# The tail of a two-branch attention kernel: last numerators in a score tile, normalized by chunk halves, half the output rows added while they are evicted

## The chip, the cores and the metric

The kernel runs on one core of a Trainium2 chip. Its engines work side by side and meet through semaphores: TensorE (PE, matmuls and their weight loads), VectorE (DVE), ScalarE (ACT), GpSimd (POOL) and SyncE (SP, which here only issues transfers). Matmul results land in PSUM, eight banks of 2 KB in each of 128 partitions; everything else lives in SBUF. The metric is the device time of one execution in microseconds, a median over several. Times inside an execution are counted from the span's start.

## The reference

One input x of 2048 tokens and 640 columns goes through two attention branches with 32 heads of 20 columns, and a gate per token mixes them:

```python
g = sigmoid((x * gate_w).sum(-1, keepdims=True))
a = A_ref(x, ...)   # linear attention, softmax feature maps, then @ A_wo
b = B_ref(x, ...)   # below, then @ B_wo
return g * a + (1 - g) * b

# B_ref: 4 segments of 512 tokens, in order, for each head
p = softmax(q @ k.T * scale + causal_mask); a_dot = p @ v
a_mem = (phi(q) @ M) / (phi(q) @ z + 1e-6)
o = sig(beta) * a_mem + (1 - sig(beta)) * a_dot
M += phi(k).T @ v; z += phi(k).sum()
```

Both outputs are of the same shape, so the sum of the two last products is formed for each block of 128 tokens (a chunk) and written out in bf16.

## The kernel before

Branch A and the projections of branch B run first. Then a loop goes over 32 steps of branch B, two at a time: segment s = 0 to 3 and group g = 0 to 7 of four heads. The order of the work on every engine is written out by hand: what is emitted first runs first on its engine (`manual_schedule`), and a plan of letters mixes projections and output rows into the steps. Waits come from the tiles: an instruction waits for what it reads, and a new tile from a pool waits until every reader of the tile that had the place is done.

PSUM is split into three pools: `bst`, two score tiles of two banks each (`st_ps`); `bnd`, one tile of two banks (`nda`); `bps`, two tiles of one bank (projections, output halves, transposes).

One step works like this. The scores of four heads go to score tiles (L666), ScalarE takes the exponential into PT tiles (L670), GpSimd clears the triangles above the diagonal (L677). `pv_items` multiplies PT with the values, which carry a column of ones, so numerators and denominators of four query chunks j and four heads i come out side by side in bank 0 of `nda` (L722, 40 matmuls, chunk j has j + 1 parts); `mem_items` puts the memory term for the same chunks into bank 1 (L730, four matmuls). `emit_epi` then works on VectorE: reciprocal of the denominators (L747), times the gates (L749), times the numerators into `td` (L759), and an add of both banks' parts into 80 columns of `oB` (L762), by GpSimd, except in the very last step, where VectorE does it.

The tail starts when the loop is over; the numerators of the last step (number 31, s = 3, g = 7) are still to be done. It makes the outputs of the last segment, chunks n = 0 to 3, each in two halves of 320 columns, written here (n, half). Each half is a sum in one PSUM bank: an identity matmul that puts in the row of branch A, which was formed earlier and lies in SBUF as bf16 (`row_mm`, L936), and five matmuls with `WoB`, one for each block of 128 columns of oB turned around (`turned_mm`, L941). Blocks 0 to 2 of oB were turned by transfers (L890) during the last steps. Block 3 (columns 384 to 511, which needs group 6, step 30) and block 4 (columns 512 to 639, which needs group 7, step 31) are turned on TensorE, and ScalarE copies them to SBUF (`block_tr`, L948 and L949). The order on TensorE before is:

- rows and blocks 0 to 2 of chunks 0 and 1 into the two score tiles, 16 matmuls (`fill`)
- numerators and memory terms of step 31 into `nda`, then its epilogue on VectorE
- block 3: four transposes, ScalarE's copy; (2,0) in a `bps` tile beside it; then block 3 of the five halves that are open
- chunk 3 in `nda`, which the epilogue must have read
- block 4: four transposes, ScalarE's copy; then block 4 of the seven halves that are open
- (2,1) in a `bps` tile, six matmuls

ScalarE and VectorE evict the halves in turn (L952, order (0,0) (0,1) (1,0) (1,1) (2,0) (3,0) (3,1) (2,1)), and SyncE's queue issues five output transfers: chunk 0, chunk 1, (2,0), chunk 3, (2,1).

Of the kernel before, what the change touches and what calls it, by code (L numbers as in the profile page):

```python
# [8 lines left out]
ALU = mybir.AluOpType  # L9
BF16 = mybir.dt.bfloat16  # L10
F32 = mybir.dt.float32
# [4 lines left out]
def kernel(  # L16
# [15 lines left out]
    nc = tc.nc  # L32
# [585 lines left out]
    with ExitStack() as bctx:  # L618
# [95 lines left out]
        def pv_items(st, js):  # L714
            vB = vBs[st.s % 2]

            def piece(j, i):
                if j == 0 and i == 0:
                    st.nda = bnd.tile([P, 2, 512], F32, name="nda")
                nd = st.nda[:, 0, 0:4 * GP].rearrange("p (j i e) -> p j i e", j=4, i=4)  # L720
                for c in range(j + 1):
                    nc.tensor.matmul(nd[:, j, i], lhsT=block(st, c)[:, i, (j - c) * P:(j - c + 1) * P],  # L722
                                     rhs=vB[:, c, 4 * st.g + i, :], start=(c == 0), stop=(c == j))
            return [(0.026 * (j + 1), lambda j=j, i=i: piece(j, i)) for j in js for i in range(4)]

        def mem_items(st):
            g = st.g

            def am(j):
                nc.tensor.matmul(st.nda[:, 1, j * GP:(j + 1) * GP], lhsT=phiq_block(st.s, g, j),  # L730
                                 rhs=Mbd[:, g].rearrange("p i e -> p (i e)"), start=True, stop=True)

            def mz(c):
                Mz = st.nda[:, 1, 4 * GP:5 * GP].rearrange("p (i e) -> p i e", i=4)
                nc.tensor.matmul(Mz, lhsT=phiks[st.s % 2][:, c, 4 * g:4 * g + 4, :],  # L735
                                 rhs=vBs[st.s % 2][:, c, 4 * g:4 * g + 4, :],
                                 start=(c == 0), stop=(c == 3))
            return ([(0.037, lambda j=j: am(j)) for j in range(4) if st.s > 0]
                    + [(0.037, lambda c=c: mz(c)) for c in range(4) if st.s < NSEG - 1]
                    + [(0.0, lambda: emit_epi(st))])  # L740

        def emit_epi(st):
            s, g = st.s, st.g
            n = 2 if s > 0 else 1
            ndv = st.nda[:, 0:n, 0:4 * GP].rearrange("p n (ji e) -> p n ji e", e=DH + 1)
            rec = bw.tile([P, 2, 16], F32, name="rec")
            nc.vector.reciprocal(out=rec[:, 0:n], in_=ndv[:, :, :, DH])  # L747
            recv = rec[:, 0:n].rearrange("p n (j i) -> p n j i", j=4)
            nc.vector.tensor_tensor(out=recv, in0=recv,  # L749
                                    in1=ogs[s][:, 0:n, :, 4 * g:4 * g + 4],  # L750
                                    op=ALU.mult)
            rb = rec[:, 0:n, :, None].to_broadcast([P, n, 16, DH])
            oview = oBs[s][:, :, g * 80:(g + 1) * 80].rearrange("p j (i d) -> p j i d", d=DH)
            if n == 1:
                nc.vector.tensor_tensor(out=oview, in0=ndv[:, 0, :, 0:DH].rearrange("p (j i) d -> p j i d", j=4),
                                        in1=rb[:, 0].rearrange("p (j i) d -> p j i d", j=4), op=ALU.mult)
            else:
                td = bw.tile([P, 2, 16, DH], F32, name="td")
                nc.vector.tensor_tensor(out=td, in0=ndv[:, :, :, 0:DH], in1=rb, op=ALU.mult)  # L759
                tdv = td.rearrange("p n (j i) d -> p n j i d", j=4)  # L760
                eng = nc.vector if st.last else nc.gpsimd
                eng.tensor_tensor(out=oview, in0=tdv[:, 0], in1=tdv[:, 1], op=ALU.add)  # L762
            if s < NSEG - 1:
                mtmp = bw.tile([P, 4, DH + 1], F32, name="mtmp")
                nc.vector.tensor_tensor(  # L765
                    out=mtmp, in0=st.nda[:, 1, 4 * GP:5 * GP].rearrange("p (i e) -> p i e", i=4),
                    in1=CM[:, g, :, :], op=ALU.mult)
                nc.gpsimd.tensor_tensor(out=Msb[:, g], in0=Msb[:, g], in1=mtmp, op=ALU.add)
                nc.gpsimd.tensor_copy(out=Mbd[:, g], in_=Msb[:, g])
# [169 lines left out]
        def turned_mm(n, half, k5s):  # L939
            for k5 in k5s:  # L940
                nc.tensor.matmul(banks[n, half], lhsT=oT4[:, n, k5, :],  # L941
                                 rhs=WoB[:, k5, half * 320:(half + 1) * 320],
                                 start=False, stop=(k5 == KC - 1))

        def block_tr(k5, eng):
            tp = bps.tile([P, 4, P], BF16, name="otp", tag="ps1")
            for n in range(4):
                nc.tensor.transpose(out=tp[:, n, :], in_=oB[:, n, k5 * P:(k5 + 1) * P], identity=ident_b)  # L948
            eng(out=oT4[:, :, k5, :], in_=tp)  # L949

        def out_half(n, half, eng):
            eng(out=rows[first + n][:, half * 320:(half + 1) * 320], in_=banks[n, half])  # L952
            lo = {(0, 1): 0, (1, 1): 0, (2, 0): 0, (3, 1): 0, (2, 1): 320}.get((n, half))
            if lo is not None:
                hs = slice(lo, (half + 1) * 320)
                nc.sync.dma_start(out=out2[(first + n) * P:(first + n + 1) * P, hs], in_=rows[first + n][:, hs])

        def fill(n):
            for half in range(2):
                row_mm(n, half)  # L960
                turned_mm(n, half, range(3))

        fill(0)
        fill(1)
        for w, fn in pv_items(prev, range(4)) + mem_items(prev):
            fn()
        block_tr(3, nc.scalar.copy)
        banks[2, 0] = bps.tile([P, 320], F32, name="o_ps", tag="ps1")
        row_mm(2, 0)
        turned_mm(2, 0, range(3))  # L970
        for n in range(2):
            for half in range(2):
                turned_mm(n, half, (3,))
        turned_mm(2, 0, (3,))
        fin = bnd.tile([P, 2, 512], F32, name="nda")
        for half in range(2):
            banks[3, half] = fin[:, half, 0:320]
            row_mm(3, half)
            turned_mm(3, half, range(4))
        block_tr(4, nc.scalar.copy)  # L980
        engs = (nc.scalar.copy, nc.vector.tensor_copy)
        order = [(0, 0), (0, 1), (1, 0), (1, 1), (2, 0), (3, 0), (3, 1)]
        for n, half in order:
            turned_mm(n, half, (4,))
        banks[2, 1] = bps.tile([P, 320], F32, name="o_ps", tag="ps1")
        row_mm(2, 1)
        turned_mm(2, 1, range(KC))
        for k, (n, half) in enumerate(order + [(2, 1)]):
            out_half(n, half, engs[k % 2])


# [28 lines left out]
```

## Time and profile before

| | us |
|---|---|
| median of 3 runs (329.59 to 329.99) | 329.69 |
| the profiled execution, whole | 329.01 |
| its span, first to last instruction | 327.3 |
| TensorE busy | 309.1 |
| ScalarE busy | 252.2 |
| VectorE busy | 222.5 |
| GpSimd busy | 212.3 |
| first row matmul of the tail (L936) starts | 313.70 |
| first numerator matmul of step 31 starts (L722) | 315.88 |
| first cast of an output half starts (L952) | 321.72 |

The granted TensorE clock was 1.00 in each stretch of the tail. In the timeline rows a number before a name is the start, then the length; `x40` says how many instructions of the same kind the row holds, from the first one's start to the last one's end; matmuls overlap, so the start of the next row says more of a group's cost than its length. Brackets name the engine's idle time before the row and what ended it. In the list of waits a row says who waited for whom, for how long in total, how often, and the longest one.

### The profile page before, as it was taken

Reading aid. Unit: us, or ns where it says so; the run is one execution under the profiler, and the core shown is the slowest. Engines: PE = TensorE matmul, PEld = TensorE weight load, DVE = VectorE, ACT = ScalarE, POOL = GpSimd, SP = SyncE. Lnnn points to the kernel's source line nnn. Section 1 sums busy time; section 2 is a strip of 40 time slices with the busy share of each in tenths; the row PEclk is TensorE's granted clock in tenths of the full one; section 3 lists DMA queues with packets and bytes.
Section 4 is the critical chain, followed back from the end, with each engine's and each line's share of the span. In section 5 each row is a group of like instructions: output and inputs, shape, how many; then the busy total and the mean of one; then the engine's idle time right before and its main releaser. Section 6 shows DMA issues by size and latency. Waiting matters only on the chain.

```text
span 327.3 us, 9498 instructions
## 1 busy us (share of the span) xinstructions
PE 309.1 (94%) x3905; PEld 213.3 (65%) x3908; DVE 222.5 (68%) x444; ACT 252.2 (77%) x321; POOL 212.3 (65%) x311
## 2 busy tenths in 40 slices
PE   7999999999999999889999999999799999999994
PEld 7788878864587788455556666655556666565562
DVE  2577988997798897377768576776566666354552
ACT  4677888148845555799999999999789888898842
POOL 8688699203178789646657676777686768665640
PEclk9999999999999999999999999999999999999999
DMA  7947935790017667756321555642555471432212
GB/s 226 211 105 188 221 97 148 215 362 10 0 35 110 129 110 110 149 105 86 59 56 34 98 57 65 123 84 49 86 91 83 87 135 27 94 80 62 49 63 80
DMA packets 91812, 34.19 MB, mean 104 GB/s; under 512 B 79866, under 2 KB 91770, under 8 KB 91770
## 3 DMA queue, kind: packets, MB, share of 16 engines
q1 hardware_dynamic: 91338, 33.11, 49.4%
q8 instruction: 30, 0.49, 0.7%
q10 hardware_dynamic: 432, 0.49, 0.6%
q14 instruction: 12, 0.10, 0.1%
HBM read 6.42 MB, written 2.62 MB: 28 GB/s over the span
## 4 chain that ended last, share of the span: by engine, by line
PE 39%; ACT 21%; DVE 2%; issue 2%; DMA 1%; SPq 0%; ACTq 0%; DVEq 0%
ACT PT L670 19%; PE st_ps L666 9%; PE proj L800 8%; PE proj L854 6%; PE nda L722 6%; PE proj L539 4%; PE num L440 2%; DMA xTf<-Eq 1%; PE nda L730 1%; PE nda L735 1%; PE st_ps L941 1%; ACT ek L826 1%; DVE oTA L952 0%; ACT oTA L949 0%; PE den L450 0%
## 5 line engine op out<-in xcount | busy, mean ns | idle before, releaser
L670 ACT ACTIVATE PT<-st_ps 128x1024 bf16<-128x1024 f32 x160 | 154.0, 1025 | 15.5 <-PE st_ps L666 13.0
L677 POOL TENSOR_SCALAR_AFFINE_SELECT PT<-PT 128x512 bf16<-128x512 bf16 (+1 forms) x130 | 87.0, 687 | 49.1 <-ACT PT L670 48.8
L722 PEld LDWEIGHTS <-PT 128*128 128x128 bf16 x1280 | 40.1, 96 | 11.2 <-issue 6.5
L722 PE MATMUL nda<-vB,PT 128*128 128x21 bf16 x1280 | 42.8, 173 | 1.5 <-DVE mtmp L765 1.3
L244 POOL TENSOR_TENSOR EkSn<-Ek,krec 128x1280 bf16<-128x1280 bf16 x16 | 37.5, 2359 | 8.3 <-DVE krec L243 8.1
L854 PEld LDWEIGHTS <-xTf 128*128 128x128 bf16 x300 | 26.3, 97 | 16.0 <-issue 7.2
L860 DVE CAST Z<-proj 128x320 bf16<-128x320 f32 x44 | 20.8, 486 | 20.1 <-PE proj L854 19.8
L232 PEld LDWEIGHTS <-xTf 128*128 128x128 bf16 x240 | 27.1, 113 | 6.2 <-DVE xTf L197 0.7
L240 DVE TENSOR_REDUCE ksum<-Ek 128x64 f32<-128x1280 bf16 x16 | 23.6, 1474 | 8.1 <-ACT Ek L236 8.1
L236 ACT ACTIVATE Ek<-pk 128x640 bf16<-128x640 f32 x32 | 20.8, 702 | 10.6 <-PE pk L232 9.8
L666 PE MATMUL st_ps<-Z 32*128 32x512 bf16 (+3 forms) x256 | 24.6, 299 | 4.3 <-ACT PT L670 3.1
L486 DVE TENSOR_TENSOR tt<-num,rr 128x640 f32<-128x640 f32 x32 | 24.8, 802 | 4.9 <-POOL rr L479 2.2
L592 POOL TENSOR_TENSOR oA<-tt 128x640 bf16<-128x640 f32 x16 | 24.6, 1546 | 4.6 <-DVE tt L486 3.4
L800 PE MATMUL proj<-WkA,oTA 128*128 128x320 bf16 x160 | 27.1, 299 | 0.0
L666 PE MATMUL st_ps<-Eq 32*128 32x512 bf16 (+3 forms) x256 | 24.5, 299 | 2.2 <-ACT PT L670 1.7
L762 POOL TENSOR_TENSOR oB<-td 128x320 bf16<-128x320 f32 x23 | 19.8, 863 | 6.9 <-DVE td L759 6.9
L398 ACT ACTIVATE Eq<-pq 128x1024 bf16<-128x1024 f32 x20 | 19.4, 1021 | 5.4 <-PE pq L393 5.4
L800 PE MATMUL proj<-WvA,oT 128*128 128x320 bf16 x120 | 22.2, 300 | 0.5 <-DVE oTA L809 0.5
L393 PE MATMUL pq<-xTf,WqA 128*128 128x512 bf16 x97 | 21.9, 379 | 0.2
L759 DVE TENSOR_TENSOR td<-nda,rec 128x640 f32<-128x640 f32 x24 | 19.8, 825 | 2.2
L539 PEld LDWEIGHTS <-xTf 128*128 128x128 bf16 x180 | 16.3, 97 | 4.4
L747 DVE RECIPROCAL rec<-nda 128x32 f32<-128x32 f32 (+1 forms) x32 | 10.6, 330 | 12.4 <-PE nda L730 6.5
(152 smaller groups left out, 558.1 us busy)
## 6 DMA issues: line engine op xcount, KB each, us to landing
Z<-EkSn SPq DMA_DIRECT2D x32, 160.0 KB, 2.7
out_dram<-orow SPq DMA_DIRECT2D x8, 160.0 KB, 2.0
out_dram<-oTA SPq DMA_DIRECT2D x7, 160.0 KB, 1.9
WvA<-in_A_wqkv_dram SPq DMA_DIRECT2D x2, 400.0 KB, 6.6
WkB<-in_B_wk_dram SPq DMA_DIRECT2D x1, 800.0 KB
WqB<-in_B_wq_dram SPq DMA_DIRECT2D x1, 800.0 KB, 6.8
WvB<-in_B_wv_dram SPq DMA_DIRECT2D x1, 800.0 KB, 8.4
WkA<-in_A_wo_dram SPq DMA_DIRECT2D x1, 800.0 KB, 11.1
```

Source lines behind the costliest of these rows:

```text
L232: nc.tensor.matmul(ps[:, bk, 0:n], lhsT=key_tokens(c, sc), rhs=rhs, start=(c == 0), stop=(c == KC - 1))
L240: nc.vector.tensor_reduce(out=ksum, in_=Ek.rearrange("p s (h f) -> p (s h) f", f=DH), axis=AX.X, op=ALU.add)
L244: nc.gpsimd.tensor_tensor(out=EkSn[:, sc].rearrange("p s (h f) -> p (s h) f", f=DH), in0=Ek.rearrange("p s (h f) -> p (s h) f", f=DH), in1 ...
L486: nc.vector.tensor_tensor(out=tt[:, sgn].rearrange("p (b h) d -> p b h d", b=2), in0=ps, in1=csb, op=ALU.mult)
L539: nc.tensor.matmul(ps, lhsT=xq[:, sc // 4, cc, sc % 4 * P:(sc % 4 + 1) * P], rhs=W[:, cc, half * 320:(half + 1) * 320], start=(cc == 0), s ...
L592: nc.gpsimd.tensor_tensor(out=oA.rearrange("p (h d) -> p h d", d=DH), in0=tt[:, 0], in1=tt[:, 1], op=ALU.add)
L666: nc.tensor.matmul(ps[:, i - i0, o:o + L - c * P], lhsT=kT[32 * i:32 * i + 32, c * P:(c + 1) * P], rhs=qT[32 * i:32 * i + 32, c * P:L], st ...
L670: nc.scalar.activation(out=PT[:, i0:i0 + 2], in_=ps, func=ACT.Exp, scale=SCALE_B)
L677: nc.gpsimd.affine_select(out=v, in_=v, pattern=[[0, n_i], [1, P]], compare_op=ALU.is_ge, fill=0.0, base=0, channel_multiplier=-1)
L722: nc.tensor.matmul(nd[:, j, i], lhsT=block(st, c)[:, i, (j - c) * P:(j - c + 1) * P], rhs=vB[:, c, 4 * st.g + i, :], start=(c == 0), stop= ...
L800: nc.tensor.matmul(ps, lhsT=oT[:, k % KC], rhs=W[:, k % KC, hs], start=(k == 0), stop=(k == n - 1))
L854: nc.tensor.matmul(ps, lhsT=xq[:, sc // 4, k, sc % 4 * P:(sc % 4 + 1) * P], rhs=W[:, k, half * 320:(half + 1) * 320], start=(k == 0), stop ...
```

## The change

All of it is in the tail and in the epilogue of step 30.

- The last step's numerators and memory terms go to the second score tile (`prev.nda = pair_ps[1]`) and not to `nda`. They come after chunk 0's seven matmuls and not after the sixteen of chunks 0 and 1. Chunk 0 of the numerators goes first, then chunks 1 to 3 for heads 0 and 1, then for heads 2 and 3.
- Chunk 1's halves go to the `nda` tile that step 30 had, after the memory terms.
- Step 30's add moves from GpSimd to VectorE.
- The last epilogue (`epi_last`) forms `td` and the sum into oB in two parts, query chunks 0 and 1, then 2 and 3.
- The transposes of block 4 come in two pairs with a copy for each. They lie in bank 0 of a score tile that takes the place of the last numerators, and (3,1) in its bank 1. (3,0) takes a `bps` tile.
- (2,1) takes the `nda` tile after chunk 1.
- For (0,1), (1,1), (3,0) and (2,1) there is no identity matmul; VectorE adds the row of branch A while it evicts. The other four halves keep theirs and are copied by ScalarE. The order of the evictions and their engines are as before.
- Chunk 3's output is issued by ScalarE's queue.

```diff
--- before.py
+++ after.py
@@ -715,7 +715,7 @@
             vB = vBs[st.s % 2]
 
             def piece(j, i):
-                if j == 0 and i == 0:
+                if j == 0 and i == 0 and not st.last:
                     st.nda = bnd.tile([P, 2, 512], F32, name="nda")
                 nd = st.nda[:, 0, 0:4 * GP].rearrange("p (j i e) -> p j i e", j=4, i=4)
                 for c in range(j + 1):
@@ -758,7 +758,7 @@
                 td = bw.tile([P, 2, 16, DH], F32, name="td")
                 nc.vector.tensor_tensor(out=td, in0=ndv[:, :, :, 0:DH], in1=rb, op=ALU.mult)
                 tdv = td.rearrange("p n (j i) d -> p n j i d", j=4)
-                eng = nc.vector if st.last else nc.gpsimd
+                eng = nc.vector if s == NSEG - 1 and g == G - 2 else nc.gpsimd
                 eng.tensor_tensor(out=oview, in0=tdv[:, 0], in1=tdv[:, 1], op=ALU.add)
             if s < NSEG - 1:
                 mtmp = bw.tile([P, 4, DH + 1], F32, name="mtmp")
@@ -948,45 +948,92 @@
                 nc.tensor.transpose(out=tp[:, n, :], in_=oB[:, n, k5 * P:(k5 + 1) * P], identity=ident_b)
             eng(out=oT4[:, :, k5, :], in_=tp)
 
-        def out_half(n, half, eng):
-            eng(out=rows[first + n][:, half * 320:(half + 1) * 320], in_=banks[n, half])
-            lo = {(0, 1): 0, (1, 1): 0, (2, 0): 0, (3, 1): 0, (2, 1): 320}.get((n, half))
-            if lo is not None:
-                hs = slice(lo, (half + 1) * 320)
-                nc.sync.dma_start(out=out2[(first + n) * P:(first + n + 1) * P, hs], in_=rows[first + n][:, hs])
-
-        def fill(n):
-            for half in range(2):
+        def epi_last(st):
+
+            s, g = st.s, st.g
+            ndv = st.nda[:, 0:2, 0:4 * GP].rearrange("p n (ji e) -> p n ji e", e=DH + 1)
+            rec = bw.tile([P, 2, 16], F32, name="rec")
+            nc.vector.reciprocal(out=rec, in_=ndv[:, :, :, DH])
+            recv = rec.rearrange("p n (j i) -> p n j i", j=4)
+            nc.vector.tensor_tensor(out=recv, in0=recv, in1=ogs[s][:, :, :, 4 * g:4 * g + 4], op=ALU.mult)
+            td = bw.tile([P, 2, 16, DH], F32, name="td")
+            oview = oBs[s][:, :, g * 80:(g + 1) * 80].rearrange("p j (i d) -> p j i d", d=DH)
+            for j in (0, 2):
+                ji = slice(4 * j, 4 * j + 8)
+                nc.vector.tensor_tensor(out=td[:, :, ji], in0=ndv[:, :, ji, 0:DH],
+                                        in1=rec[:, :, ji, None].to_broadcast([P, 2, 8, DH]), op=ALU.mult)
+                tdv = td[:, :, ji].rearrange("p n (j i) d -> p n j i d", j=2)
+                nc.vector.tensor_tensor(out=oview[:, j:j + 2], in0=tdv[:, 0], in1=tdv[:, 1], op=ALU.add)
+
+        SUMMED = {(0, 1), (1, 1), (3, 0), (2, 1)}
+
+        def fill(n, half, k5s):
+
+            own = (n, half) not in SUMMED
+            if own:
                 row_mm(n, half)
-                turned_mm(n, half, range(3))
-
-        fill(0)
-        fill(1)
-        for w, fn in pv_items(prev, range(4)) + mem_items(prev):
+            for k5 in k5s:
+                nc.tensor.matmul(banks[n, half], lhsT=oT4[:, n, k5, :],
+                                 rhs=WoB[:, k5, half * 320:(half + 1) * 320],
+                                 start=(k5 == 0 and not own), stop=(k5 == KC - 1))
+
+
+        prev.nda = pair_ps[1]
+        for half in range(2):
+            fill(0, half, range(3))
+        for w, fn in pv_items(prev, (0,)):
             fn()
+        later = pv_items(prev, (1, 2, 3))
+        for i0 in (0, 2):
+            for j in range(3):
+                for i in (i0, i0 + 1):
+                    later[4 * j + i][1]()
+        for w, fn in mem_items(prev)[:4]:
+            fn()
+        epi_last(prev)
+        first_nda = bnd.tile([P, 2, 512], F32, name="nda")
+        for half in range(2):
+            banks[1, half] = first_nda[:, half, 0:320]
+            fill(1, half, range(3))
         block_tr(3, nc.scalar.copy)
         banks[2, 0] = bps.tile([P, 320], F32, name="o_ps", tag="ps1")
-        row_mm(2, 0)
-        turned_mm(2, 0, range(3))
-        for n in range(2):
-            for half in range(2):
-                turned_mm(n, half, (3,))
-        turned_mm(2, 0, (3,))
-        fin = bnd.tile([P, 2, 512], F32, name="nda")
-        for half in range(2):
-            banks[3, half] = fin[:, half, 0:320]
-            row_mm(3, half)
-            turned_mm(3, half, range(4))
-        block_tr(4, nc.scalar.copy)
-        engs = (nc.scalar.copy, nc.vector.tensor_copy)
-        order = [(0, 0), (0, 1), (1, 0), (1, 1), (2, 0), (3, 0), (3, 1)]
-        for n, half in order:
+        fill(2, 0, range(3))
+        for n, half in ((0, 0), (0, 1), (1, 0), (1, 1), (2, 0)):
+            turned_mm(n, half, (3,))
+        last_ps = bst.tile([P, 2, L], F32, name="st_ps")
+        tp = last_ps[:, 0].bitcast(BF16)[:, 0:4 * P].rearrange("p (n t) -> p n t", n=4)
+        banks[3, 0] = bps.tile([P, 320], F32, name="o_ps", tag="ps1")
+        banks[3, 1] = last_ps[:, 1, 0:320]
+
+        def last_tr(n):
+            nc.tensor.transpose(out=tp[:, n, :], in_=oB[:, n, 4 * P:KC * P], identity=ident_b)
+
+        last_tr(0)
+        last_tr(1)
+        nc.scalar.copy(out=oT4[:, 0:2, 4, :], in_=tp[:, 0:2])
+        fill(3, 0, range(4))
+        last_tr(2)
+        last_tr(3)
+        nc.scalar.copy(out=oT4[:, 2:4, 4, :], in_=tp[:, 2:4])
+        for n, half in ((0, 0), (0, 1), (1, 0), (1, 1)):
             turned_mm(n, half, (4,))
-        banks[2, 1] = bps.tile([P, 320], F32, name="o_ps", tag="ps1")
-        row_mm(2, 1)
-        turned_mm(2, 1, range(KC))
-        for k, (n, half) in enumerate(order + [(2, 1)]):
-            out_half(n, half, engs[k % 2])
+        fill(3, 1, range(4))
+        for n, half in ((2, 0), (3, 0), (3, 1)):
+            turned_mm(n, half, (4,))
+        banks[2, 1] = bnd.tile([P, 2, 512], F32, name="nda")[:, 0, 0:320]
+        fill(2, 1, range(KC))
+        out_to = {(0, 1): (nc.sync, 0, 0), (1, 1): (nc.sync, 1, 0), (2, 0): (nc.sync, 2, 0),
+                  (3, 1): (nc.scalar, 3, 0), (2, 1): (nc.sync, 2, 320)}
+        for n, half in ((0, 0), (0, 1), (1, 0), (1, 1), (2, 0), (3, 0), (3, 1), (2, 1)):
+            row = rows[first + n][:, half * 320:(half + 1) * 320]
+            if (n, half) in SUMMED:
+                nc.vector.tensor_tensor(out=row, in0=banks[n, half], in1=row, op=ALU.add)
+            else:
+                nc.scalar.copy(out=row, in_=banks[n, half])
+            if (n, half) in out_to:
+                eng, n, lo = out_to[n, half]
+                hs = slice(lo, (half + 1) * 320)
+                eng.dma_start(out=out2[(first + n) * P:(first + n + 1) * P, hs], in_=rows[first + n][:, hs])
 
 
 # ---- launch: one core; inputs and outputs as the reference has them ----
```

## The prediction

> **What bounds the kernel now.** I read the page's head and its chain first, then the timeline from 311 us on, engine by engine, then the waits of that stretch and the transfers.
>
> ```profile
> span 327.3 us, 9498 instructions
> PE 39%; ACT 21%; DVE 2%; issue 2%; DMA 1%; SPq 0%; ACTq 0%; DVEq 0%
> ```
>
> The chain is mostly TensorE (PE) work. The change touches nothing that starts before about 311 us, so only the tail matters. TensorE's rows there (start, length, line, operation, tiles, count):
>
> ```profile
> 313.70 0.30 PE L936 MATMUL st_ps<-oTA,ident_b 128*128 128x320 bf16 x1
> ...
> 315.88 1.16 PE L722 MATMUL nda<-vB,PT 128*128 128x21 bf16 x40
> 316.89 0.31 PE L730 MATMUL nda<-Mbd,xTf 128*128 128x84 bf16 x4
> 317.03 0.39 PE L948 MATMUL otp<-ident_b,oB 128*128 128x128 bf16 x4
> 317.26 0.30 PE L936 MATMUL o_ps<-oTA,ident_b 128*128 128x320 bf16 x1
> ...
> 318.10 0.72 PE L941 MATMUL st_ps<-WvA,oTA 128*128 128x320 bf16 x4
> ...
> 321.24 0.72 PE L941 MATMUL st_ps<-WvA,oTA 128*128 128x320 bf16 x4 [0.68 <-ACT oTA L949]
> ...
> 322.33 0.84 PE L941 MATMUL o_ps<-WvA,oTA 128*128 128x320 bf16 x5
> ```
>
> TensorE is one stream with two holes, each behind a ScalarE copy of transposes (before 318.10 and before 321.24); its last matmul ends at 322.33 + 0.84 = 323.17. Then the other engines:
>
> ```profile
> 312.91 1.68 POOL L677 TENSOR_SCALAR_AFFINE_SELECT PT<-PT 128x256 bf16<-128x256 bf16 x4 [0.26 <-ACT PT L670]
> 314.74 0.82 DVE L759 TENSOR_TENSOR td<-nda,rec 128x640 f32<-128x640 f32 x1
> 315.65 0.86 POOL L762 TENSOR_TENSOR oB<-td 128x320 bf16<-128x320 f32 x1 [1.05 <-DVE td L759]
> 317.23 0.36 DVE L747 RECIPROCAL rec<-nda 128x32 f32<-128x32 f32 x1 [1.67 <-PE nda L730]
> 317.63 0.19 DVE L749 TENSOR_TENSOR rec<-rec,Eq 128x32 f32<-128x32 f32 x1
> 317.92 0.82 DVE L759 TENSOR_TENSOR td<-nda,rec 128x640 f32<-128x640 f32 x1
> 318.78 0.49 DVE L762 TENSOR_TENSOR oB<-td 128x320 bf16<-128x320 f32 x1
> ...
> 317.46 0.59 ACT L949 COPY oTA<-otp 128x512 bf16<-128x512 bf16 x1 [3.70 <-PE otp L948]
> 321.72 0.75 ACT L952 CAST oTA<-st_ps 128x320 bf16<-128x320 f32 x2 [0.54 <-PE st_ps L941]
> 322.18 0.89 DVE L952 CAST oTA<-st_ps 128x320 bf16<-128x320 f32 x2 [2.90 <-ACT oTA L952]
> 323.38 0.48 DVE L952 CAST oTA<-o_ps 128x320 bf16<-128x320 f32 x1
> 323.50 0.43 ACT L952 CAST oTA<-nda 128x320 bf16<-128x320 f32 x1 [0.69 <-DVE oTA L952]
> ```
>
> The last eviction, (2,1) by VectorE (DVE), ends at 323.86. The output transfers on the sync engine's queue (SP) come behind it:
>
> ```profile
> 322.69 2.28 SPq L956 DMA_DIRECT2D out_dram<-oTA  x5
> 324.59 0.38 SPq L956 DMA_DIRECT2D out_dram<-oTA  x1
> DMA to landing us min/median/max: 1.7/1.8/1.9
> SPq L1015 <- DMA out_dram<-oTA: 1.3, 2, 1.0
> ```
>
> The first row is all five issues; their starts run from 322.69 to 324.59, so (324.59 - 322.69) / 4 = 0.48 us each. The data of the fifth is ready at 323.86, yet it is issued 0.73 us later, behind the fourth. The last row says that the final wait is for an output's landing. So the end is: last issue at 324.59, 1.7 us to land, about 1 us of closing. **Whatever moves the last issue moves the end.**
>
> **The change, part by part.** Prices first. Sixteen 320-column matmuls fill 313.70 to 315.88: 0.136 each. The 40 numerator matmuls take 315.88 to 316.89: 1.01. Four memory-term matmuls: 0.14. Four transposes: 317.03 to 317.26, 0.23; ScalarE's copy starts 0.43 after the first of them, and a matmul starts 0.05 after the copy's end.
>
> *Row matmuls.* Four of eight identity matmuls go (L936): 4 x 0.136 = 0.54 us of TensorE. The addition moves into VectorE's eviction, which becomes a tensor_tensor from a PSUM and a bf16 operand:
>
> ```profile
> 312.74 0.49 DVE L809 TENSOR_TENSOR oTA<-proj,oTA 128x320 bf16<-128x320 f32 x1 [1.31 <-PE proj L800]
> ```
>
> That is the very operation, 0.49 against 0.48 for the cast: free.
>
> *Numerators in a score tile.* They no longer wait for the nda tile (read until 314.74 + 0.82 = 315.56), so 7 matmuls instead of 16 stand ahead of them: 313.70 + 7 x 0.136 = 314.65. They need GpSimd's (POOL's) four triangles, which end at 312.91 + 1.68 = 314.59. The second pair of heads, which needs the last two triangles, comes only after 4 + 18 matmuls, at about 315.21, so 0.6 us covers it; without that cover each us of triangles would cost one. Numerators end at 315.66, memory terms at 315.80. The two banks of chunk 1 follow in the freed nda tile (7 matmuls, to 316.75), long after 315.56.
>
> *The add of step 30, GpSimd to VectorE.* VectorE: 315.60 to 316.09 (0.49) instead of GpSimd's 315.65 to 316.51. The transposes of block 3 that need it come at 316.75, after either. What is queued behind it on VectorE is the last step's reciprocal, which could start at 315.66 + 0.34 = 316.00 and now starts at 316.1. Cover for this 0.1 us: 0.4 us of slack, below.
>
> *Block 3.* Transposes 316.75, copy 317.18 to 317.77, the four matmuls of (2,0) beside it to 317.52, then a hole, and at 317.82 five matmuls, to 318.50.
>
> *Last epilogue by halves.* By the rows, product 0.40 after the reciprocal's start and td 0.29 after that: 316.10, 316.50, 316.80. Half a td is 320 elements, as in the 0.49 rows; the step from 320 to 640 costs 0.33, so an add of 160 is estimated at 0.32. td 316.80 to 317.29, add to 317.65, td to 318.15, add to 318.51. The bound from above is that a half costs what the whole does (0.82 and 0.49): then td ends at 319.0 and the last add at 319.5. I take the estimate, since 0.49 is measured on this size. The score tile is then free at 318.15, 0.35 us before TensorE needs it at 318.50.
>
> *Block 4 in two pairs.* Copies of 256 columns: 512 take 0.59 and 320 take 0.43, so 0.38. Transposes 318.50, first copy 318.81 to 319.19. Meanwhile (3,0), four matmuls, runs from 318.62 to 319.16. The second pair writes the bank that the first copy reads, so it waits until 319.24; copy 319.55 to 319.93. Behind it on TensorE the four last matmuls of chunks 0 and 1: 319.36 to 319.90. Then (3,1): it lies in the other half of the tile that the second copy reads. The waits show how halves of one PSUM tile are treated:
>
> ```profile
> DVE oTA L952 <- ACT oTA L952: 2.9, 1, 2.9
> ACT oTA L952 <- DVE oTA L952: 0.7, 1, 0.7
> ```
>
> VectorE's first cast waits for ScalarE's cast of the other half, and (3,1) waits in the same way for (3,0). I therefore let (3,1) wait for the copy: 319.98 to 320.66 (bound from below: 0.08 earlier). Three matmuls more: 321.07.
>
> *Evictions.* ScalarE's come 0.32 apart (0.75 for two of 0.43), VectorE's 0.41. (0,0) behind the copy 319.90 to 320.33, (0,1) 320.36 to 320.85, (1,0) to 320.65, (1,1) 320.77 to 321.25.
>
> *The new wait.* (2,1) now takes the nda tile, which holds chunk 1 until 321.25. TensorE has no work left behind it and would have been there at 321.07. It starts at 321.31 and takes 0.84 for five matmuls: 322.15. VectorE adds from 322.18 to 322.67, and the issue follows at 322.70.
>
> *Queues.* SP issues at 320.88, 321.36, 321.84 and is idle at 322.3. Chunk 3 goes by ScalarE's queue once (3,0) and (3,1) are out: (3,1) ends on TensorE at about 321.25, ScalarE's copy after (2,0) at 321.77, so the issue is at 321.8. That queue's earlier rows (source line 96):
>
> ```profile
> L96 ACTq DMA_DIRECT2D wnat_k<-in_A_wqkv_dram x3: 427/450/454, 0.8 to 1.7; - x3
> DMA to landing us min/median/max: 2.9/3.9/4.8
> wnat_k<-in_A_wqkv_dram SPq DMA_DIRECT2D x2, 160.0 KB, 4.1
> out_dram<-oTA SPq DMA_DIRECT2D x2, 80.0 KB, 1.7
> out_dram<-oTA SPq DMA_DIRECT2D x7, 160.0 KB, 1.9
> ```
>
> An issue is 0.45. For landing I take 1.9, the output row of that size, and keep 4.8 as the bound; with 1.9 it lands at 323.7, before (2,1)'s 322.70 + 1.7 = 324.4.
>
> Left on SP, chunk 3 would go at 322.32 and (2,1) at 322.80: the other queue itself is worth 0.1 us. The 1.7 of (2,1) was measured with a 160 KB transfer issued 0.48 ahead of it, so company is in the price.
>
> The Trainium skill (DMA: Bandwidth & Descriptors, Issuing engines are not separate DMA queues) says that transfers from all queues share the same engines and interleave, so that a second queue saves issue time alone. By that rule 80 KB of chunk 3 could still be in front of (2,1)'s bytes; the rows price 80 KB at 1.9 - 1.7 = 0.2, which would make 328.0 of the sum below. The trace as far as it goes has no such delay at 0.48 us distance, and here it is 0.9.
>
> **The sum.** Last issue 324.59 to 322.70: -1.89 us, of which 0.70 is the queue delay (0.73 to 0.03) and 1.19 the earlier last eviction (323.86 to 322.67). The profiled execution took 329.01 us (span 327.3), so 327.12; the median of the runs, 329.69, lies 0.68 above it: **327.8 us**.
>
> **Rivals.**
> *Halves leave side by side.* If ScalarE and VectorE may read the two halves of a tile at once, (1,1) is out by about 320.80, (2,1) starts at 321.07, and 0.24 more is won: 327.6. The two waits above speak against it. The Trainium skill (PSUM — Partial Sum Buffer, PSUM bank collisions raise a hardware error) says that only engines on one bank of a quadrant collide; by that rule the halves, a bank each, need no wait. The trace here shows them waiting.
> *VectorE becomes the bound.* With whole prices for the half operations the score tile comes free at 319.0 instead of 318.15, TensorE's transposes slip from 318.50 to 319.1, and everything after with them: 0.6 lost, 328.4.
> *ScalarE's queue lands late (the other side).* At 4.8 us the transfer issued at 321.8 lands at 326.6, after today's 324.59 + 1.7 = 326.3: 0.3 slower, 330.0; at the median 3.9 it is 329.1. From 4.5 us on the change loses, from 5.2 by more than 0.2%. For it: the only rows of that queue. Against: those were loads at the start, where SP's like loads took 4.1 too.
> *The change doesn't do it:* a wait that the rows can't show sits in the new order of tiles, worth 1.2 us or more.
>
> **How the numbers follow.** 0.2% is 0.66 us, about what a measurement of this kernel can tell from no change. My sum 72% (its own range 327.4 to 328.2); halves side by side 6%; VectorE as bound 9%; late queue 8% (5 within 0.2%, 3 slower); unseen wait 5% (1 within, 4 slower). Faster 87, same 6, slower 7. The range reaches from the halves' 327.6 less the 0.08 of (3,1) and 0.3 of scatter (the three runs shown lie 0.4 apart), 327.2, to VectorE's 328.4 and the same 0.3, 328.7.
>
> **What would show it.** Numerators from about 314.65 and no hole before them; VectorE's add of step 30 ahead of the last reciprocal; transposes of block 4 in two pairs at about 318.5 and 319.2; (2,1)'s five matmuls after a short hole that VectorE's eviction ends, at 321.3; the last SP issue within 0.1 us of the last eviction's end, at about 322.7. I am wrong if TensorE stands before the first transposes of block 4, or if the last wait is for ScalarE's transfer.

## The result and the profile after

| | before | after |
|---|---|---|
| median, us | 329.84 (329.59 to 330.24, 4 runs) | 327.01 (326.66 to 327.39, 4 runs) |
| profiled execution, us | 329.01 | 326.66 |
| its span, us | 327.3 | 324.9 |
| first identity matmul (L936) starts | 313.70 | 313.38 |
| last output issue starts, counted from there | 10.88 | 8.92 |
| span's end, counted from there | 13.60 | 11.56 |

The ratio of after to before is 0.9924, with a 95% interval of 0.9902 to 0.9946: faster by 0.5 to 1.0%. The forecast was 327.8, with a range of 327.2 to 328.7; the median lies 0.8 below the forecast and 0.2 below the range's lower end; by the ratio, 0.9924 of the 329.69 shown before is 327.2, that end itself.

Since the change touches the tail alone, the tail is the measure from here on: the time from the start of the first identity matmul to the start of the last output issue. It is free of what happens earlier. The first matmul's row, and the main rows of TensorE's timeline behind it, for the kernel after:

```profile
313.38 0.30 PE L936 MATMUL st_ps<-oTA,ident_b 128*128 128x320 bf16 x1
313.52 0.98 PE L976 MATMUL st_ps<-WvA,oTA 128*128 128x320 bf16 x6
314.33 1.15 PE L722 MATMUL st_ps<-vB,PT 128*128 128x21 bf16 x40
315.34 0.31 PE L730 MATMUL st_ps<-Mbd,xTf 128*128 128x84 bf16 x4
...
316.44 0.39 PE L948 MATMUL otp<-ident_b,oB 128*128 128x128 bf16 x4
316.66 0.30 PE L936 MATMUL o_ps<-oTA,ident_b 128*128 128x320 bf16 x1
316.80 0.57 PE L976 MATMUL o_ps<-WvA,oTA 128*128 128x320 bf16 x3
317.50 0.45 PE L941 MATMUL st_ps<-WvA,oTA 128*128 128x320 bf16 x2
...
318.19 0.28 PE L1009 MATMUL st_ps<-ident_b,oB 128*128 128x128 bf16 x2
318.30 0.71 PE L976 MATMUL o_ps<-WvA,oTA 128*128 128x320 bf16 x4
318.93 0.27 PE L1009 MATMUL st_ps<-ident_b,oB 128*128 128x128 bf16 x2
...
319.66 0.30 PE L936 MATMUL st_ps<-oTA,ident_b 128*128 128x320 bf16 x1
...
320.61 0.30 PE L941 MATMUL st_ps<-WvA,oTA 128*128 128x320 bf16 x1
320.91 0.84 PE L976 MATMUL nda<-WvA,oTA 128*128 128x320 bf16 x5
```

The numerators stand behind seven matmuls, and nothing stops TensorE before them. Four holes are left, each a start that comes later than the 0.136 us per matmul would have it: 0.29 before 317.50 (block 3's copy), 0.09 before 318.93 and 0.08 before 319.66 (the copies of block 4), 0.17 before 320.91 ((2,1) waits for its tile). Then the evictions and the issues of the kernel after, from each engine's timeline:

```profile
319.23 0.37 ACT L1017 COPY oTA<-st_ps 128x256 bf16<-128x256 bf16 x1 [0.36 <-PE st_ps L1009]
319.50 0.43 ACT L1032 CAST oTA<-st_ps 128x320 bf16<-128x320 f32 x1
...
320.99 0.43 ACT L1032 CAST oTA<-st_ps 128x320 bf16<-128x320 f32 x1
321.45 0.35 ACTq L1036 DMA_DIRECT2D out_dram<-oTA  x1
...
319.97 0.49 DVE L1030 TENSOR_TENSOR oTA<-st_ps,oTA 128x320 bf16<-128x320 f32 x1 [1.98 <-ACT oTA L1032]
320.38 0.48 DVE L1030 TENSOR_TENSOR oTA<-nda,oTA 128x320 bf16<-128x320 f32 x1
320.81 0.49 DVE L1030 TENSOR_TENSOR oTA<-o_ps,oTA 128x320 bf16<-128x320 f32 x1
321.79 0.49 DVE L1030 TENSOR_TENSOR oTA<-nda,oTA 128x320 bf16<-128x320 f32 x1 [0.49 <-PE nda L976]
...
320.48 2.15 SPq L1036 DMA_DIRECT2D out_dram<-oTA  x4
...
322.31 0.33 SPq L1036 DMA_DIRECT2D out_dram<-oTA  x1
```

The last issue stands 0.03 us behind the last eviction (321.79 + 0.49 = 322.28), where it stood 0.73 behind before. The tail's gain splits by its own chain:

| | before | after | gain |
|---|---|---|---|
| TensorE's last matmul ends, counted from the first identity matmul | 323.17 - 313.70 = 9.47 | 321.75 - 313.38 = 8.37 | 1.10 |
| from there to the last eviction's end | 0.69 | 0.53 | 0.16 |
| from there to the last issue | 0.73 | 0.03 | 0.70 |
| sum | 10.89 | 8.93 | 1.96 |

(The sums are 0.01 above the times in the first table, by rounding.) Most of TensorE's 1.10 us can be read from its rows. Four matmuls fewer are 0.54. Behind block 4's transposes TensorE stood for 0.84 us before (320.17 + 0.23 = 320.40 to 321.24); now chunk 3's matmuls come behind the transposes and cover the copies, and 0.09 + 0.08 = 0.17 is left. The new wait before (2,1) takes 0.17 back.

### The profile page after: what moved, and what is told of

Its sections match the earlier page's. It is cut to its first block, busy times and chain, and to the rows that moved or that the text cites. A ratio compares the mean times of both kernels' runs of the same rounds, so it can differ in the third digit from the quotient of the medians.

```text
span 324.9 us, 9495 instructions
## 1 busy us (share of the span) xinstructions
PE 308.9 (95%) x3904; PEld 212.9 (66%) x3904; DVE 223.0 (69%) x447; ACT 252.1 (78%) x322; POOL 211.2 (65%) x310
## 4 chain that ended last, share of the span: by engine, by line
PE 41%; ACT 20%; issue 2%; DVE 1%; DMA 1%; SPq 0%; ACTq 0%; DVEq 0%
ACT PT L670 19%; PE st_ps L666 9%; PE proj L800 8%; PE proj L854 7%; PE nda L722 6%; PE proj L539 4%; PE num L440 2%; DMA xTf<-Eq 1%; PE nda L730 1%; PE nda L735 1%; ACT ek L826 1%; PE nda L976 1%; PE st_ps L976 0%; PE den L450 0%; DVE rec L747 0%
## 5 line engine op out<-in xcount | busy, mean ns | idle before, releaser
L722 PE MATMUL nda<-vB,PT 128*128 128x21 bf16 x1240 | 41.7, 173 | 1.4 <-DVE mtmp L765 0.9
L762 POOL TENSOR_TENSOR oB<-td 128x320 bf16<-128x320 f32 x22 | 18.9, 861 | 5.9 <-DVE td L759 4.9
L759 DVE TENSOR_TENSOR td<-nda,rec 128x640 f32<-128x640 f32 x23 | 19.0, 825 | 2.1
L232 PE MATMUL pk<-WkA,xTf 128*128 128x320 bf16 x120 | 18.3, 299 | 0.6 <-DVE xTf L197 0.6
```

Source lines behind the costliest of these rows:

```text
L232: nc.tensor.matmul(ps[:, bk, 0:n], lhsT=key_tokens(c, sc), rhs=rhs, start=(c == 0), stop=(c == KC - 1))
```

## The experiments

Each kernel is the changed one with the edit shown; the last three combine several. The tail comes from each kernel's own trace.

| kernel | tail expected by the theory | tail measured | whole, median us |
|---|---|---|---|
| the changed kernel | | 8.92 | 327.01 |
| changed kernel again | 8.9 | 8.92 | 327.06 |
| chunk 3 on the sync engine's queue | 8.97 | 8.99 | 327.29 |
| whole last epilogue | 8.92 | 8.92 | 327.09 |
| identity matmuls back | 9.4 | 9.39 | 328.26 |
| numerators behind chunk 1 | 9.2 to 9.4 | 9.31 | 327.56 |
| block 4 with one copy | 9.13 | 9.15 | 327.39 |
| step 30's add on GpSimd | 8.92 | 8.92 | 327.51 |
| chunk 1 finished first | 8.75 | 8.76 | 327.07 |
| block 3 early | 8.63 | 8.62 | 327.47 |
| both | 8.46 | 8.45 | 327.30 |
| both, (2,0) summed | 8.4 to 8.5 | 8.35 | 327.14 |
| the same again | 8.35 | 8.35 | 327.01 |

**The changed kernel again.** Only a comment is added.

> The changed kernel once more, nothing but a comment added. The measure in all of these runs is the tail: from the start of the first identity matmul (chunk 0's row) to the start of the last output issue, 10.89 us before (324.59 - 313.70) and 8.92 after (322.30 - 313.38). Theory: the change is worth 1.97 us in the tail and nothing elsewhere, so the tail is 8.9 again and the whole is faster than before by about 2.0 us, at most 2.3; the further 0.3 us that the profiled execution had won before its tail began is scatter. Rival: the stretch before the tail became faster as well, then the whole is faster by 2.6 us or more again and the tail again begins about 0.3 us earlier.

The tail is 8.92 again, and it began at 313.51, 0.19 earlier than in the kernel before. The whole was 327.06 us against 329.31 for the kernel before on the same chip, 2.25 less; ratio 0.9930 (0.9917 to 0.9943), that is 1.9 to 2.7 us. The tail to the span's end is 2.04 shorter (13.60 to 11.56). The theory fits, though the interval reaches the rival's 2.6. Against the rival stands that in ten of the thirteen traces with a changed tail the tail began later than the 313.70 of the kernel before. The first comparison's 2.83 had some luck in it; where from is taken up at the end of this section.

**The second queue.**

```diff
-                  (3, 1): (nc.scalar, 3, 0), (2, 1): (nc.sync, 2, 320)}
+                  (3, 1): (nc.sync, 3, 0), (2, 1): (nc.sync, 2, 320)}
```

> Chunk 3's output goes back to the sync engine's queue, everything else as changed. Theory: issues are 0.48 us apart, and with (0), (1), (2,0) at 320.48, 320.91, 321.39 the fourth follows at 321.87 and is over by 322.27, so the last issue waits at most until 322.35: tail 8.92 + 0.05, no measurable change. Rival (the second queue is what took away the 0.73 us of queue delay): the last issue comes a full issue later, tail 9.4 or more.

Tail 8.99. The sync engine's timeline of this run has its last three issues end to end, the last one, at 321.97 + 1.37 - 0.38 = 322.96, only 0.10 us behind its data (322.86):

```profile
321.97 1.37 SPq L1036 DMA_DIRECT2D out_dram<-oTA  x3
```

So the second queue is worth 0.07 us here, and it isn't what took the 0.73 us of queue delay away. On one queue the issues start 0.43 to 0.50 us apart, so five of them need 1.9 us from the first start to the last. Before, the first started at 322.69 and the last data were ready only 1.17 us later (323.86), so the row of issues ran on behind them. Its fourth and fifth:

```profile
324.09 0.88 SPq L956 DMA_DIRECT2D out_dram<-oTA  x2
```

Chunk 3, the fourth, was out at 323.50 + 0.43 = 323.93 and had to wait for the queue too. Now the first issue starts at 320.48, 1.80 us ahead of the last data (322.28), and the row of issues is all but done when those come. Counted from the first identity matmul, the first issue came 1.89 us earlier (7.10 instead of 8.99) and the last eviction's end 1.26 (8.90 instead of 10.16). This is read from the rows; no run brings the delay back by itself.

**The halves of the epilogue.**

```diff
-            for j in (0, 2):
-                ji = slice(4 * j, 4 * j + 8)
+            for j in (0,):
+                ji = slice(0, 16)
...
-                nc.vector.tensor_tensor(out=oview[:, j:j + 2], in0=tdv[:, 0], in1=tdv[:, 1], op=ALU.add)
+                nc.vector.tensor_tensor(out=oview, in0=tdv[:, 0], in1=tdv[:, 1], op=ALU.add)
```

> The last epilogue in one piece (one product of 640 elements, one add of 320), everything else as changed. Theory: by the rows, td would run 316.37 to 317.19 and the add to 317.72; the first transposes of block 4 come at 318.19 and need the score tile free and oB written, both done by then, so the tail stays 8.92. VectorE even has one fixed cost less. Rival: the halves let the transposes start earlier, then without them the tail is longer by about 0.3 us.

Tail 8.92: the halves are worth nothing in this order of the work. In one piece the sum is even written earlier than in two, 4.34 instead of 4.61 us after the first identity matmul, with two instructions fewer. Both end ahead of the transposes, which come at 4.81 either way. The changed kernel's second td, the last reader of the score tile, ends at 317.62, 0.57 us ahead of them:

```profile
317.14 0.48 DVE L963 TENSOR_TENSOR td<-st_ps,rec 128x320 f32<-128x320 f32 x1
```

**The identity matmuls.**

```diff
-        SUMMED = {(0, 1), (1, 1), (3, 0), (2, 1)}
+        SUMMED = set()
+        ON_VECTOR = {(0, 1), (1, 1), (3, 0), (2, 1)}
...
-            if (n, half) in SUMMED:
-                nc.vector.tensor_tensor(out=row, in0=banks[n, half], in1=row, op=ALU.add)
+            if (n, half) in ON_VECTOR:
+                nc.vector.tensor_copy(out=row, in_=banks[n, half])
```

> All eight identity matmuls are back, VectorE only copies. Theory: TensorE's stream sets the tail, and the rows of (0,1), (1,1) and (2,1) lie on it at 0.136 each, that of (3,0) partly in a hole of 0.09: tail 8.92 + 0.46 = 9.4. Rival (TensorE waits for others in the tail, and its own work hides): tail within 0.1 of 8.92.

Tail 9.39: four matmuls of 0.136 us cost 0.47 of their 0.54, as laid out. It is the largest effect that undoing one edit shows. The whole is slower still: the profiled execution took 327.98 us, 1.32 more than the changed kernel's 326.66, because its tail also began late, at 314.21 and not 313.38. The median, 328.26, comes from six runs that lie far apart (327.70 to 328.81).

**The score tile.**

```diff
-        prev.nda = pair_ps[1]
-        for half in range(2):
-            fill(0, half, range(3))
+        prev.nda = bnd.tile([P, 2, 512], F32, name="nda")
+        for n in range(2):
+            for half in range(2):
+                fill(n, half, range(3))
...
-        last_ps = bst.tile([P, 2, L], F32, name="st_ps")
+        last_ps = bnd.tile([P, 2, 512], F32, name="nda")
...
-        banks[2, 1] = bnd.tile([P, 2, 512], F32, name="nda")[:, 0, 0:320]
+        banks[2, 1] = bst.tile([P, 2, L], F32, name="st_ps")[:, 0, 0:320]
```

Chunk 1's later `fill` in the nda tile goes too.

> The last numerators stay in the nda tile, behind chunk 1 as before (14 matmuls ahead of them, not 7); chunk 1 stays in the second score tile, block 4's transposes and (3,1) take the nda tile after the epilogue, and (2,1) takes a score tile. Counted from the first identity matmul: numerators 1.90 instead of 0.95, block 3's transposes at 3.05 as now, but the last reciprocal at 3.26 instead of 2.31, so that the tile is free at 5.19 and block 4's transposes come at 5.25 instead of 4.81. Theory (the score tile buys the epilogue its cover): 0.44 lost there; (2,1) finds the score tile of chunk 0 free and wins back 0.17, or that of chunk 1 and wins nothing: tail 9.2 to 9.4, against 8.92. Rival (the epilogue was never on the path, as in the kernel before, where it ended 0.9 us ahead of the transposes): tail 8.75 to 8.92.

Tail 9.31. TensorE's timeline of this run shows the price, and the small gain that (2,1) gives back by taking the score tile of chunk 0, which is free by then:

```profile
318.49 0.30 PE L941 MATMUL o_ps<-WvA,oTA 128*128 128x320 bf16 x1
319.07 0.28 PE L1006 MATMUL nda<-ident_b,oB 128*128 128x128 bf16 x2 [0.28 <-DVE td L963]
...
321.49 0.30 PE L941 MATMUL nda<-WvA,oTA 128*128 128x320 bf16 x1
321.63 0.84 PE L976 MATMUL st_ps<-WvA,oTA 128*128 128x320 bf16 x5
```

TensorE stands idle until VectorE's td is done with the tile: the transposes start at 5.35 (319.07 - 313.72) instead of 4.81, 0.10 more than I had worked out, since the numerators began at 2.00 (315.72 - 313.72) and not at 1.90. The 0.17 us hole before (2,1) is gone. With the numerators 1.05 us later, the epilogue becomes the bound. The run moves three tiles together, so its 0.39 us is the price of the whole arrangement; what the other parts would bring with late numerators was not tried.

**Block 4 with one copy.**

```diff
-        nc.scalar.copy(out=oT4[:, 0:2, 4, :], in_=tp[:, 0:2])
-        fill(3, 0, range(4))
         last_tr(2)
         last_tr(3)
-        nc.scalar.copy(out=oT4[:, 2:4, 4, :], in_=tp[:, 2:4])
+        nc.scalar.copy(out=oT4[:, :, 4, :], in_=tp)
+        fill(3, 0, range(4))
```

> Block 4 goes in one piece again: four transposes, one copy of 512 columns, with (3,0) beside it. Theory: the copy runs from 5.24 to 5.82 (counted from the first identity matmul), the last matmuls of chunks 0 and 1 start at 5.87 instead of 5.66, and the evictions and (2,1) follow 0.21 later: tail 9.13. Rival (the pairs only move the hole, since the second pair waits for the first copy anyway): tail 8.92.

Tail 9.15: the two pairs are worth 0.23 us. The copy runs 0.59 us in this run and the last matmuls of chunk 0 start behind it, at 5.87 instead of 5.66 (319.76 - 313.89 against 319.04 - 313.38).

**Step 30's add.**

```diff
-                eng = nc.vector if s == NSEG - 1 and g == G - 2 else nc.gpsimd
-                eng.tensor_tensor(out=oview, in0=tdv[:, 0], in1=tdv[:, 1], op=ALU.add)
+                nc.gpsimd.tensor_tensor(out=oview, in0=tdv[:, 0], in1=tdv[:, 1], op=ALU.add)
```

> Step 30's add goes back to GpSimd. Theory: it ends there at about 316.2 on the changed kernel's clock, 0.2 us before block 3's transposes at 316.44, and the last reciprocal is set by the memory terms, so the tail stays 8.92. Rival (block 3 waits for oB): tail longer by 0.1 to 0.4.

Tail 8.92: no effect. In that run's timelines GpSimd adds and TensorE's transposes of block 3 follow, 0.25 us after its end (315.72 + 0.86 = 316.58):

```profile
315.72 0.86 POOL L761 TENSOR_TENSOR oB<-td 128x320 bf16<-128x320 f32 x1 [1.06 <-DVE td L759]
316.83 0.39 PE L947 MATMUL otp<-ident_b,oB 128*128 128x128 bf16 x4
```

The move would matter in the next experiment but one, where block 3's transposes start 0.4 us earlier.

**(2,1)'s wait.**

```diff
-        for n, half in ((0, 0), (0, 1), (1, 0), (1, 1)):
+        for n, half in ((1, 0), (1, 1), (0, 0), (0, 1)):
             turned_mm(n, half, (4,))
...
-        for n, half in ((0, 0), (0, 1), (1, 0), (1, 1), (2, 0), (3, 0), (3, 1), (2, 1)):
+        for n, half in ((1, 0), (1, 1), (0, 0), (0, 1), (2, 0), (3, 0), (3, 1), (2, 1)):
```

> Chunk 1 gets its last matmuls and its evictions ahead of chunk 0. Theory: (2,1)'s new wait is for the eviction of (1,1), which now ends about 0.4 us earlier, so TensorE goes on without a hole (now 0.17 us): tail 8.75. Rival (the last issue is set by VectorE's row of evictions and not by (2,1)'s wait): tail 8.92.

Tail 8.76. The new wait of the change was a wait for the eviction of (1,1), and it costs 0.16 us.

**Block 3's hole.**

```diff
             fill(1, half, range(3))
-        block_tr(3, nc.scalar.copy)
+            if half == 0:
+                block_tr(3, nc.scalar.copy)
```

> Block 3's transposes come between the two halves of chunk 1 instead of behind them. Theory: the seven matmuls left, (1,1) and (2,0), take 0.95 us and cover ScalarE's copy, so the hole of 0.29 us in TensorE's stream goes, and everything behind moves up by it: tail 8.63 against 8.92. The last epilogue's tile is free 0.3 us before the transposes of block 4 need it. Rival (the epilogue or the evictions become the bound as soon as TensorE is earlier): tail 8.8 to 8.92.

Tail 8.62. TensorE's timeline of this run, from the transposes to block 3's first matmuls:

```profile
316.74 0.39 PE L948 MATMUL otp<-ident_b,oB 128*128 128x128 bf16 x4
316.96 0.57 PE L976 MATMUL nda<-WvA,oTA 128*128 128x320 bf16 x3
317.37 0.30 PE L936 MATMUL o_ps<-oTA,ident_b 128*128 128x320 bf16 x1
317.51 0.57 PE L976 MATMUL o_ps<-WvA,oTA 128*128 128x320 bf16 x3
317.91 0.43 PE L941 MATMUL st_ps<-WvA,oTA 128*128 128x320 bf16 x2
```

Seven matmuls now cover ScalarE's copy and the hole is gone. The transposes start at 2.65 (316.74 - 314.09). With GpSimd's add, at 2.80 in the run above (316.58 - 313.78), they would have waited; VectorE's is done in time. That was read from two runs, not tried together.

**Both, and one sum more.** The last variant adds this to the two edits above:

```diff
-        SUMMED = {(0, 1), (1, 1), (3, 0), (2, 1)}
+        SUMMED = {(0, 1), (1, 1), (2, 0), (3, 0), (2, 1)}
```

> Block 3's transposes between the halves of chunk 1, and chunk 1 finished and evicted ahead of chunk 0. Theory: the two holes add, 0.29 + 0.17: tail 8.46, whole faster than the changed kernel by 0.14%, and than the one before by 0.75 to 0.85%. Rival: one of the two holes comes back as another, tail 8.6 to 8.75.

> As the run with both, and (2,0) without its identity matmul as well, added by VectorE. Theory: TensorE wins 0.136 us more, but VectorE then has five evictions 0.41 us apart; the fifth can start at about 7.93, where (2,1) is ready at 7.80, so almost nothing is left: tail 8.4 to 8.5, VectorE the bound. Rival (TensorE stays the bound): tail 8.32.

The tails are 8.45 and 8.35. The two holes add up. In the second my theory was wrong by a little: VectorE keeps up, and 0.10 of the 0.136 us is won. The rest is lost at block 3, where a small hole comes back: without (2,0)'s identity matmul the three matmuls from 317.72 end their turn at 318.13, and block 3's first matmul starts at 318.15, 0.05 after ScalarE's copy (317.51 + 0.59). VectorE's last two rows in that run:

```profile
321.42 0.88 DVE L1031 TENSOR_TENSOR oTA<-o_ps,oTA 128x320 bf16<-128x320 f32 x2
322.27 0.49 DVE L1031 TENSOR_TENSOR oTA<-nda,oTA 128x320 bf16<-128x320 f32 x1
```

VectorE ends the pair at 322.30 and has begun the last add at 322.27; TensorE's last matmul ended at 321.39 + 0.84 = 322.23. The two are level, so a sixth sum should no longer pay; it was not tried.

Both variants have a shorter tail than either kernel, but the whole does not show it: the ratios to before are 0.9929 (0.9910 to 0.9948) and 0.9923 (0.9901 to 0.9946), beside 0.9930 for the changed kernel. Half a microsecond is the size of these intervals, and the tails began late in these runs.

**The start of the tail.**

> The fastest variant (both holes closed, (2,0) summed as well) once more, with a comment added. Its tail began at 314.44, later than in the changed kernel (313.38, 313.51), and so its 0.57 us shorter tail does not show in the whole. Theory: the start of the tail scatters from execution to execution, because waits for transfers in the unchanged part land a little earlier or later; then it begins anywhere between 313.3 and 314.5 now, the tail is 8.35 again, and the whole lies between 326.3 and 327.4. Rival: the place of the instructions in the program makes the head of this variant slower; then the tail begins at 314.3 to 314.5 again.

The tail is 8.35 again, the whole 327.01 us (ratio 0.9927, 0.9913 to 0.9940), and the tail began at 314.28. That lies within the theory's range and 0.02 below the rival's, and so does not settle it. The wholes speak for the rival: the spans of nine timed executions of the changed kernel (324.9 to 326.0) and of nine of this variant (325.1 to 325.7) have medians of 325.4 and 325.3, though this variant's tail is 0.57 us shorter in both of its traces. Scatter alone would let the difference show, so the head of this variant seems to be slower by about half a microsecond; why is not shown, and the comparison goes across chips, on which the kernel before took 329.3 to 329.8. There is scatter as well, as the width of both ranges says. What the traces do show is one place where the kernels differ: TensorE's weight loads wait at the start of the loop over the steps, for nothing that the profile names. The wait's row from 128 to 136 us (total, times, longest) for four kernels: before, changed, the last variant, and its repetition:

```profile
PEld L666 <- issue: 1.9, 3, 1.0
```

```profile
PEld L666 <- issue: 1.4, 3, 0.7
```

```profile
PEld L666 <- issue: 1.4, 2, 1.2
```

```profile
PEld L666 <- issue: 1.1, 2, 0.8
```

The longest wait (1.0, 0.7, 1.2, 0.8) goes with the time that the stretch from about 92 to 134 us takes (41.93, 41.39, 42.10, 41.76 us between the same two ScalarE instructions, in the same order of kernels). Over all fourteen traces the longest wait goes from 0.65 to 1.24 us, and the stretch rises with it from 41.39 to 42.17. One program had 1.2 and 0.8 in two executions, so at least this part changes from execution to execution. What it waits for stays open.

## Why the prediction was right, and where it was off

Counted from the first identity matmul, as the prediction's own numbers are when 313.70 is taken off:

| step | predicted | measured |
|---|---|---|
| numerators start | 0.95 | 0.95 |
| block 3's transposes | 3.05 | 3.06 |
| block 4's first and second pair of transposes | 4.80, 5.54 | 4.81, 5.55 |
| (3,1) starts, behind the second copy | 6.28 | 6.28 |
| (2,1) starts | 7.61 | 7.53 |
| last eviction ends | 8.97 | 8.90 |
| last issue | 9.00 | 8.92 |

- **Numerators in a score tile:** right, with the triangles' cover as said. GpSimd's last triangle ended at 313.50 + 0.77 = 314.27, and the second pair of heads came about 0.6 us later.
- **Row matmuls and VectorE's add:** right; the add took 0.48 to 0.49, as the price from L809 said. All on the path but for a hole, by the run with the rows back.
- **Step 30's add:** right that it costs and brings nothing here.
- **Halves of the epilogue:** the price of a half was right (0.49 and 0.32), but the slack was 0.57 us where the prediction had 0.35, because the reciprocal started 0.09 earlier (2.31 and not 2.40) and the second td 0.08 before the add ahead of it ended. The prediction did not say that with this slack the halves bring nothing; the run did.
- **Halves of one PSUM tile wait for each other:** right. VectorE's first add starts at 319.97, when ScalarE's cast of the other half (319.50 + 0.43) is over, and (3,1) waits for the copy. The rival in which they leave side by side is out. By the Trainium skill's rule (PSUM — Partial Sum Buffer, PSUM bank collisions raise a hardware error) the two banks could be used at once. Chunk 3 of the kernel after agrees: (3,0) and (3,1) lie in two tiles but go into the same output row, and ScalarE's cast of (3,1) starts at 320.99, while VectorE's add of (3,0) runs from 320.81 to 321.30. So the wait goes with the shared PSUM tile and not with the shared row. That it is put in by the kernel's own semaphores fits this, but no run took them away within one tile.
- **(2,1)'s wait:** right in kind, 0.08 us early in time, because ScalarE starts an instruction 0.10 before the one ahead ends also between a copy and a cast; the prediction had 0.03. That is the whole error of the tail.
- **ScalarE's queue:** worth 0.07, predicted 0.1. Its transfer landed in 2.1 us and not 1.9, far from the 4.8 of the rival that ends slower. The last one, (2,1), landed in 1.6 us beside it (1.7 before), so the 0.2 us for bytes of chunk 3 in front of it did not show. It was down at 321.45 + 2.1 = 323.55, the last one at 322.31 + 1.6 = 323.9. The transfers' rows after:

```profile
out_dram<-oTA SPq DMA_DIRECT2D x2, 80.0 KB, 1.8
out_dram<-oTA ACTq DMA_DIRECT2D x1, 160.0 KB, 2.1
```

- **VectorE as bound:** did not happen; the epilogue becomes one only with numerators that come later, and with five sums the evictions are level with TensorE. Neither sign of being wrong showed: TensorE goes on to block 4's transposes without a hole, and the last landing is (2,1)'s.
- **The step that was off** is the last one of the sum, from the span to the median: "the median of the runs, 329.69, lies 0.68 above it". The tail's gain was 1.96 (forecast 1.89), but the profiled execution began its tail 0.32 earlier as well and its last transfer landed 0.06 sooner, and the median after lay only 0.35 above its profiled execution (327.01 to 326.66). Together that is 0.07 + 0.32 + 0.06 + 0.33 = 0.78 of the 0.79 us between 327.8 and 327.01; the larger part of it is luck and not the change. With the repetition the gain is 2.25 us, where the tail accounts for 2.04.

## What to carry to other kernels

At the end of a kernel, follow each engine's rows from the first instruction that changes and count from there: durations and hand-over gaps of the old trace gave every start on the chain of the new order to within 0.1 us, while the total scattered by several tenths. Of several edits made together, find by single undoing which ones are on the chain: here saved matmuls, early numerators and the two copies were, and the halved epilogue, the add's move and the second queue were not, or hardly. The single effects need not make up the whole: here they add to 0.47 + 0.39 + 0.23 + 0.07 = 1.16 of 1.96 us, and the shorter wait in the queue belongs to no single edit. A row of issues on one queue takes its time from the first one, so the first output must be ready early enough, and a tile that is taken over late is worth arranging so that its readers finish first.

## What the runs showed of the hardware

- Two transfers issued within 0.1 us on two queues both took longer: in the kernel after, the 160 KB one on ScalarE's queue 2.1 us and the 80 KB one on SyncE's queue 1.9, against 1.9 and 1.7 when issued about 0.5 us apart on one queue (the kernel before, and the run with chunk 3 back on SyncE's queue). In the run with five sums they were issued 0.34 apart and took 1.8 and 1.7. A gain of issue time is partly given back, though here not on the path. The Trainium skill (DMA: Bandwidth & Descriptors, Issuing engines are not separate DMA queues) says that transfers from all queues share the same engines; these times agree.
- ScalarE's instructions of 0.43 us follow each other 0.32 apart and VectorE's of 0.49 us 0.41 apart when nothing makes them wait. A chain of evictions has to be counted by the distance, not by the length.
- The unchanged stretch before the tail ended anywhere between 313.38 and 314.44 us in the fourteen traces, a range half as wide as the whole gain of the change.
